# Two output blocks built in place of their summands, and the last entry's products reordered so that a plain copy comes last

## The chip, the cores and the metric

The kernel runs on one core of a Trainium2 chip. The metric is device time in microseconds for one execution, as the median of several runs. The core has TensorE (matrix products, PE in the profile; its weight loads are PEld), VectorE (DVE), ScalarE (ACT) and GpSimd (POOL). They run side by side, each through its own list of instructions in order, and wait for each other by semaphores. SyncE (SP) issues the transfers between memory and the core.

## The reference

The reference is attention through 32 packed queries per head, followed by a gated feed-forward layer that mixes over the sequence:

```
p_packed = softmax(p k^T / 8) v                       # per entry (8) and head (8)
x        = softmax(q p_packed^T / 8) p_packed         # 576 rows x 512
h        = relu(x @ w_in);  u, v = halves of h        # 512 + 512 columns
v_n      = (v - mean(v)) / sqrt(var(v) + 1e-6)        # per row
v_s      = w_spatial @ v_n + b_spatial                # mixes the 576 rows
out      = (u * v_s) @ w_out                          # 512 x 512
```

The change touches the last line alone, the product with `w_out`.

## The kernel before

The kernel goes through the eight entries of the batch one after the other (loop at line 1108 for entries 1 to 7; entry 0 is written out ahead of it). For each entry there is an `Attention` object, and a `FeedForward` object `ff` for the second half. While the products of one entry run, parts of the attention of later entries are put between them (`nxt`, `far`, `further`); for the last entry `nxt` is None and nothing is left to put there. The instructions of TensorE, VectorE, ScalarE and GpSimd stay in the order in which they are written (`InOrder`, `PIN`). The stores and loads are issued by SyncE, in one queue.

fp32 products are made from fp32r matmuls: an operand is split into a high part (`block_hi`, a rounding copy on ScalarE) and a low part (`block_lo`, a subtraction on VectorE), and each product sums high*high, high*low and low*high. In `product` (line 718) that is 12 matmuls of 128x288: for each half `f` of the output first four that read the high part of the moving operand, then two that read its low part.

For entries 1 to 7 the product with `w_out` is not made of eight block products but of seven (the Winograd form of Strassen's scheme). The gated activations `u` form four blocks g11, g12, g21 and g22 (features x sequence halves), the weights A11, A12, A21, A22 with the sums S1 to S4, the activations the differences T1 to T4 (`block_sum`, line 686, each made from an earlier one: T2 from T1, T4 from T2). With P1 = A11 g11, the output blocks of 256 features x 288 positions are

- block 11 = P1 + A12 g21. Both products are summed in the same PSUM tile, so `out11` is only a copy on ScalarE.
- block 12 = U + S4 g22 (summed onto S1 T1), where U = P1 + S2 T2.
- block 21 = U + A22 T4 (summed onto S3 T3).
- block 22 = U + P57, where P57 = S1 T1 + S3 T3; both are in the core's memory (SBUF).

P1, P5 and P57 live in one tile `prod` with the tag `v_h`, U in one with the tag `v_l` (`part`, line 741). The pool has one buffer for each of these tags. The next entry uses the same memory for its tiles `v_h` and `v_l`, the parts of the normalised activations, which it writes in `norm_hi` and `norm_lo`.

Each output block is made in an `o` tile (`out_block`, line 759, two buffers, tag "o") and stored from it by `put` (line 762):

```python
        def out_block(self):
            return two.tile([P, 2, HS], F32, tag="o", name="o")
```

A buffer is free again when the store that reads it has landed. Per entry four output blocks and the small tile `part` of the next entry's `relu(2)` (line 550, first instruction of ScalarE there) go through the two buffers in turn. The last lines of an entry are 1212 to 1250: after the seventh product (`A22`) entries 1 to 6 make block 22, then block 21; the last entry makes block 21 in two halves, each stored by itself, and then block 22.

The PSUM tiles of the four accumulators are `on(turns[0])` to `on(turns[3])`, that is all eight banks; each half `f` of a product lies in a bank of its own.

Of the kernel before, what the change touches and what calls it, by code (L numbers as in the profile page):

```python
# [14 lines left out]
ALU = mybir.AluOpType  # L15
# [8 lines left out]
HS = S // 2  # L24
# [25 lines left out]
def body(ctx: ExitStack, tc, q, k, v, vt, p, w_in, w_sp, b_sp, w_out, out):  # L50
# [11 lines left out]
    pe, dve, act, pool = (  # L62
        InOrder(tc, e) if x in PIN else e
        for e, x in ((nc.tensor, "t"), (nc.vector, "v"), (nc.scalar, "s"), (nc.gpsimd, "g"))
    )
# [6 lines left out]
    psum = ctx.enter_context(tc.tile_pool(name="ps", bufs=1, space=bass.MemoryType.PSUM))  # L72

    def on(i):

        return lambda: psum.tile([P, 2, 512], F32, tag=f"ps{i}", name=f"ps{i}_t")

    def by_turns(*quarters):
        turn = itertools.cycle([on(i) for i in quarters])
        return lambda: next(turn)()  # L80
# [25 lines left out]
    def load_k(b):  # L106
        pT = two.tile([P, NJ * NP], F32, tag="pT", name="pT")
        nc.sync.dma_start(pT, p[:, b, :])
        loaded["p", b] = pT
        kT = io.tile([P, 2, NJ, HS], F32, tag="kT", name="kT")  # L110
        for x in parts(b):
            nc.sync.dma_start(kT[:, x], k[b, :, x])
        loaded["k", b] = kT

    def load_v(b):
        v_sb = io.tile([P, NC + 1, H * D], F32, tag="v", name="v_sb")
        nc.sync.dma_start(v_sb[:, :NC, :], v[b])
        nc.sync.dma_start(v_sb[:TAIL, NC, :], vt[b])
        loaded["v", b] = v_sb

    def load_q(b):
        qT = io.tile([P, 2, NJ, HS], F32, tag="qT", name="qT")
        for x in parts(b):
            nc.sync.dma_start(qT[:, x], q[b, :, x])
        loaded["q", b] = qT
# [105 lines left out]
    A11, A12, A22, S1, S2, S3, S4, A21 = range(8)  # L231
# [265 lines left out]
    class FeedForward:  # L497
# [268 lines left out]
        def out_whole(self, k, f, t):  # L766
            o = self.out_block()
            act.copy(o, self.ds[k][:, :, :HS])
            self.put(o, f, t)

        def out11(self):
            self.out_whole(A12, 0, 0)

# [2 lines left out]
            self.add_part(o, "U", S4)  # L776
            self.put(o, 0, 1)

        def out21(self, fs=slice(0, 2)):
            if fs.start == 0:  # L780
                self.o21 = self.out_block()
            self.add_part(self.o21, "U", A22, fs)
            self.put(self.o21, 1, 0, fs)

        def out22(self):
            o = self.out_block()
            dve.tensor_tensor(o, self.part("U"), self.part("P57"), op=ALU.add)
            self.put(o, 1, 1)

# [15 lines left out]
    att, nxt, far, further = (Attention(b) for b in range(4))  # L807
    keep_warm(2, 9)
    att.pack_scores(by_turns(0, 3))
    ff = FeedForward(0, att)  # L810
# [297 lines left out]
    for b in range(1, B):  # L1108
        att, nxt, far = nxt, far, further
        further = Attention(b + 3) if b + 3 < B else None  # L1110
        ff = FeedForward(b, att)
        ff.value(2, psum=on(q0))
        ff.value(0, psum=on(q1))
        ff.relu(2)
        ff.value(1, psum=on(q2))
        ff.relu(0)
        ff.relu_tail()
        ff.stats(2)
        ff.inverse(2)
        ff.stats(0)  # L1120
        ff.inverse(0)
        ff.relu(1)
        if far:
            far.pack_turn(on(q3), ff.ps[2])
        if nxt:
            nxt.packed_turn(ff.ps[2])
            nxt.packed_turned()
        if far:
            far.pack_turned()
        ff.stats(1)  # L1130
        ff.inverse(1)
        ff.norm(2)
        ff.norm(0)
        ff.up(0, psum=on(q1))
        ff.up_relu(0)
        ff.norm_hi(0)
        ff.norm(1)
        ff.norm_lo(0)
        ff.up(1, psum=on(q2))
        ff.norm_hi(2)  # L1140
        ff.up_relu(1)
        ff.up(2, psum=on(q0))
        ff.up_relu(2)
        ff.tail_hi()
        ff.norm_lo(2)
        ff.up(3, psum=on(q3))
        ff.up_relu(3)
        ff.norm_hi(1)
        if nxt:
            nxt.query_scores(psum=by_turns(q1, q2))  # L1150
            nxt.query_tiles()
            if far:
                load_q(b + 2)
            nxt.mix(1, psum=on(q0))
            nxt.query_spread(0)
            nxt.query_spread(1)
            nxt.mix_hi(1)
            if far:
                far.pack_values(on(q3))
                far.packed()  # L1160
                if further:
                    load_v(b + 3)
            nxt.mix_lo(1)
        ff.norm_lo(1)
        if nxt:
            nxt.mix(0, psum=on(q1))
            nxt.mix_hi(0)
            if further:
                further.pack_scores(psum=by_turns(q2, q3))
                if b + 4 < B:  # L1170
                    load_k(b + 4)
                for r in range(2):
                    further.pack_max(r)
                    further.pack_exp(r)
            nxt.mix_lo(0)
            nxt.query_max(0)
            nxt.query_sub(0)
            nxt.query_exp(0)
            if further:
                further.pack_sum()  # L1180
        if further:
            turns = (q0, q1, q2, q3)
        else:
            turns = (q3, q2, q0, q1) if nxt else (q1, q2, q0, q3)
        if not nxt:
            for cs in ((0, 1), (2, 3)):
                ff.gate((0, 1), "hm", cs, psum=by_turns(*turns[:2]))
        for e, i in enumerate(turns):
            ff.gate((e,), "hmlt" if nxt or e > 1 else "lt", psum=on(i))
            if nxt and e == 1:  # L1190
                nxt.query_sum(0)
                nxt.query_norm(0)
            ff.gated(e)
            if nxt and e == 0:
                nxt.query_max(1)
                nxt.query_sub(1)
                nxt.query_exp(1)
            elif e == 1:
                ff.block_hi("g11")
                ff.block_sum("T1")  # L1200
                ff.block_hi("T1")
                ff.block_lo("g11")
                if nxt:
                    nxt.query_turn(0)
                    nxt.query_hi(0)
                ff.block_lo("T1")
            elif nxt and e == 2:
                nxt.query_lo(0)
                nxt.query_tail(0)
                nxt.query_sum(1)  # L1210
                nxt.query_norm(1)
        ff.product(A11, "g11", psum=on(turns[0]))
        ff.block_hi("g21")
        ff.block_sum("T3")
        ff.block_lo("g21")
        ff.keep_part("P1", A11)
        ff.block_hi("g22")
        ff.block_sum("T2")
        ff.product(S1, "T1", psum=on(turns[1]))
        ff.block_hi("T3")  # L1220
        ff.block_lo("g22")
        ff.keep_part("P5", S1)
        ff.block_lo("T3")
        ff.block_hi("T2")
        ff.product(A12, "g21", onto=A11)
        ff.out11()
        ff.block_sum("T4")
        ff.block_lo("T2")
        ff.block_hi("T4")
        ff.product(S4, "g22", onto=S1)  # L1230
        ff.block_lo("T4")
        if nxt:
            nxt.query_turn(1)
            nxt.query_hi(1)
        ff.product(S3, "T3", psum=on(turns[2]))
        ff.add_part("P57", "P5", S3)
        if nxt:
            nxt.query_lo(1)
            nxt.query_tail(1)
        ff.product(S2, "T2", psum=on(turns[3]))  # L1240
        ff.add_part("U", "P1", S2)
        ff.out12()
        ff.product(A22, "T4", onto=S3)
        if nxt:
            ff.out22()
            ff.out21()
        else:
            for f in range(2):
                ff.out21(slice(f, f + 1))
            ff.out22()  # L1250
        q0, q1, q2, q3 = turns[0], turns[1], turns[3], turns[2]


# [52 lines left out]
```

## Time and profile before

| what | us |
|---|---|
| median of three timed runs (408.6 to 409.56) | 409.43 |
| profiled execution, its own time | 407.98 |
| its span | 406.2 |
| TensorE busy (matmul) | 394.9 |
| VectorE busy | 332.9 |
| ScalarE busy | 192.7 |
| GpSimd busy | 74.1 |

The span counts from the first instruction of the program to its last; the profiled execution's own time is 1.78 us longer than the span. The granted TensorE clock was 0.996 of full speed over the execution. Matmuls overlap, so the duration of one (0.29 us) is longer than the time from one start to the next (0.13 us); the starts are what counts. In a row of the timeline the first number is the start in us from the span's start, the second the duration; where several instructions of one kind follow closely they are merged, with their count behind the x.

### The profile page before, as it was taken

To read this page: it belongs to the slowest core of one execution; us is meant where nothing else is said; L and a number is where in the kernel's file an instruction comes from. 1 tells how busy PE (TensorE), PEld (TensorE's weight loads), DVE (VectorE), ACT (ScalarE), POOL (GpSimd) and SP (SyncE) were. 2 spreads that over 40 slices of the span, in tenths; PEclk is the share of its full clock that TensorE was granted. 3 is DMA by queue.
4 is the path that set the end of the run, shared out by engine and by line. 5 is a ranking of instruction groups with operands and counts; after the bars stand their busy time and mean duration, and the time that the engine had idled before them with its cause. 6 is when DMAs were issued, how large, how long until landed. Compare 5 with 4: busy or idle time off the path is not lost.

```text
span 406.2 us, 8936 instructions
## 1 busy us (share of the span) xinstructions
PE 394.9 (97%) x3800; PEld 354.5 (87%) x3800; DVE 332.9 (82%) x567; ACT 192.7 (47%) x291; POOL 74.1 (18%) x98
## 2 busy tenths in 40 slices
PE   7999999999999999999999999999999999999993
PEld 5768977799799879999699888999799889999993
DVE  2597799979799779977899788995899789978563
ACT  3587865766435353434634273244634272526140
POOL 1566445644000120002100030001200030004000
PEclk9999999999999999999999999999999999999998
DMA  7999057730810227020530205002300200020002
GB/s 306 382 383 397 20 178 305 241 116 2 293 66 31 87 81 278 2 85 34 224 129 31 87 13 225 0 29 89 120 0 30 87 2 2 0 102 17 2 30 88
DMA packets 16620, 46.62 MB, mean 115 GB/s; under 512 B 1346, under 2 KB 10562, under 8 KB 13764
## 3 DMA queue, kind: packets, MB, share of 16 engines
q1 hardware_dynamic: 16580, 46.05, 31.1%
q8 instruction: 30, 0.49, 0.5%
q14 instruction: 10, 0.08, 0.1%
HBM read 36.61 MB, written 9.44 MB: 113 GB/s over the span
## 4 chain that ended last, share of the span: by engine, by line
PE 94%; DVE 3%; POOL 1%; issue 1%; DMA 1%; POOLq 0%; DVEq 0%
PE ps_t L43 94%; DVE nmax L43 1%; POOL bits L43 1%; DMA out_t<-o 1%; DVE bits L43 0%; DVE t L43 0%; DVE o L43 0%; DVE sm_t L43 0%; DVE w_in_sb L43 0%; DVE pp L43 0%; DVE mx L43 0%; DVE prod L43 0%; POOL ident masks.py:199 0%; DVE rtot L43 0%; POOL ident masks.py:197 0%
## 5 line engine op out<-in xcount | busy, mean ns | idle before, releaser
L43 PE MATMUL ps_t<-wsp_h,v_h 128*128 128x288 f32 x256 | 55.9, 300 | 0.0
L43 PE MATMUL ps_t<-wsp_l,v_h 128*128 128x288 f32 x256 | 54.5, 295 | 0.0
L43 POOL TENSOR_TENSOR rstd<-mv,eps 128x2 f32<-128x2 f32 (+2 forms) x26 | 6.9, 265 | 245.5 <-DVE mv L43 245.4
L43 PE MATMUL ps_t<-t,wout_h 128*128 128x288 f32 x232 | 48.3, 294 | 0.0
L43 PEld LDWEIGHTS ps_t<-wsp_h,v_h 128*128 128x128 f32 x256 | 40.8, 188 | 3.8 <-DVE m_l L43 1.9
L43 PEld LDWEIGHTS ps_t<-wsp_l,v_h 128*128 128x128 f32 x256 | 41.5, 189 | 0.0
L43 ACT CAST g_h<-u 128x576 fp32r<-128x576 f32 x24 | 16.1, 674 | 49.4 <-DVE u L43 49.1
L43 PE MATMUL ps_t<-wsp_h,v_l 128*128 128x288 f32 x256 | 39.4, 296 | 0.0
L43 PEld LDWEIGHTS ps_t<-t,wout_h 128*128 128x128 f32 x232 | 38.0, 188 | 0.0
L43 PEld LDWEIGHTS ps_t<-wsp_h,v_l 128*128 128x128 f32 x256 | 35.9, 189 | 0.5 <-issue 0.5
L43 PE MATMUL ps_t<-t,wout_l 128*128 128x288 f32 x116 | 32.3, 294 | 0.0
L43 PE MATMUL ps_t<-g_h,wout_h 128*128 128x288 f32 x104 | 30.1, 305 | 0.6 <-DVE pp L43 0.6
L43 PE MATMUL ps_t<-g_h,wout_l 128*128 128x288 f32 x104 | 29.1, 295 | 0.0
L43 PE MATMUL ps_t<-a_h,m_h 128*128 128x288 f32 x128 | 28.1, 301 | 0.0
L43 PE MATMUL ps_t<-a_h,m_l 128*128 128x288 f32 x128 | 27.4, 296 | 0.0
L43 PE MATMUL ps_t<-a_l,m_h 128*128 128x288 f32 x128 | 27.4, 296 | 0.0
L43 DVE TENSOR_TENSOR u<-ps_t,u 128x576 f32<-128x576 f32 x28 | 21.0, 749 | 7.3 <-PE ps_t L43 7.3
L43 PE MATMUL ps_t<-m_l,a_h 128*128 128x512 f32 x80 | 25.8, 390 | 0.0
L43 PE MATMUL ps_t<-m_h,a_h 128*128 128x512 f32 x80 | 25.8, 391 | 0.0
L43 ACT ACTIVATE sm_t<-sm_t 128x576 f32<-128x576 f32 x16 | 11.0, 685 | 27.5 <-DVE sm_t L43 23.7
L43 DVE TENSOR_TENSOR o<-ps_t,prod 128x576 f32<-128x576 f32 (+1 forms) x15 | 10.7, 717 | 15.4 <-DMA out_t<-o 15.1
L43 ACT COPY part<-ps_t 64x512 f32<-64x512 f32 x8 | 4.7, 583 | 39.2 <-DVE o L43 39.2
(136 smaller groups left out, 989.6 us busy)
## 6 DMA issues: line engine op xcount, KB each, us to landing
out_t<-o SPq DMA_DIRECT2D x31, 288.0 KB, 2.3
v_sb<-in_v SPq DMA_DIRECT2D x8, 1024.0 KB, 8.1
qT<-in_q SPq DMA_DIRECT2D x7, 1152.0 KB, 5.4
kT<-in_k SPq DMA_DIRECT2D x7, 1152.0 KB, 8.4
raw<-in_w_in SPq DMA_DIRECT2D x4, 1024.0 KB, 12.7
raw<-in_w_out SPq DMA_DIRECT2D x2, 1024.0 KB, 9.8
kT<-in_k SPq DMA_DIRECT2D x2, 576.0 KB
qT<-in_q SPq DMA_DIRECT2D x2, 576.0 KB, 12.8
```

The lines of the kernel that those rows point to most:

```text
L43: return lambda *a, **k: self.tc.keep_in_program_order(call(*a, **k))
```

## The change

`out22` adds U into P57 in place and stores from there; `out21` adds the seventh product into U in place and stores from there. Neither takes an `o` tile any more. Blocks 11 and 12 still do. The end of an entry moves into two methods: `down` for entries 1 to 6, in the order of before, and `last_down` for entry 7, in another order: the products are A11, S1, S2, S3, S4, A22, A12 (before: A11, S1, A12, S4, S3, S2, A22), the splits and sums follow that order, the stores go 12, 22, 21, and block 11 comes last, copied and stored in two halves (`out11_split`).

```diff
+        def out11_split(self):
+            o = self.out_block()
+            for i in range(2):
+                act.copy(o[:, i], self.ds[A12][:, i, :HS])
+                self.put(o, 0, 0, slice(i, i + 1))
...
-        def out21(self, fs=slice(0, 2)):
-            if fs.start == 0:
-                self.o21 = self.out_block()
-            self.add_part(self.o21, "U", A22, fs)
-            self.put(self.o21, 1, 0, fs)
+        def out21(self):
+
+            o = self.part("U")
+            self.add_part(o, "U", A22)
+            self.put(o, 1, 0)
 
         def out22(self):
-            o = self.out_block()
-            dve.tensor_tensor(o, self.part("U"), self.part("P57"), op=ALU.add)
+
+            o = self.part("P57")
+            dve.tensor_tensor(o, self.part("U"), o, op=ALU.add)
             self.put(o, 1, 1)
+
+        def down(self, turns, nxt):
...
+            self.product(A22, "T4", onto=S3)
+            self.out22()
+            self.out21()
+
+        def last_down(self, turns):
+
+            self.product(A11, "g11", psum=on(turns[0]))
+            self.block_sum("T2")
+            self.block_hi("T2")
+            self.block_sum("T3")
+            self.block_hi("T3")
+            self.block_lo("T2")
+            self.keep_part("P1", A11)
+            self.product(S1, "T1", psum=on(turns[1]))
+            self.block_hi("g22")
+            self.block_lo("T3")
+            self.block_lo("g22")
+            self.keep_part("P5", S1)
+            self.block_sum("T4")
+            self.block_hi("T4")
+            self.product(S2, "T2", psum=on(turns[3]))
+            self.add_part("U", "P1", S2)
+            self.block_hi("g21")
+            self.product(S3, "T3", psum=on(turns[2]))
+            self.block_lo("T4")
+            self.add_part("P57", "P5", S3)
+            self.block_lo("g21")
+            self.product(S4, "g22", onto=S1)
+            self.out12()
+            self.out22()
+            self.product(A22, "T4", onto=S3)
+            self.out21()
+            self.product(A12, "g21", onto=A11)
+            self.out11_split()
...
         if nxt:
-            ff.out22()
-            ff.out21()
+            ff.down(turns, nxt)
         else:
-            for f in range(2):
-                ff.out21(slice(f, f + 1))
-            ff.out22()
+            ff.last_down(turns)
```

## Rows read from the trace of the kernel before

**Rows 1.** The page, busy us by engine, share of the span, instructions.
```profile
PE 394.9 (97%) x3800; PEld 354.5 (87%) x3800; DVE 332.9 (82%) x567; ACT 192.7 (47%) x291; POOL 74.1 (18%) x98
```

**Rows 2.** The chain that ended last: start us, us, what.
```profile
74.13 324.15 PE ps_t L43 x2922
...
399.87 2.26 DMA out_t<-o
...
402.23 0.76 DVE o L43
```

**Rows 3.** Waits of VectorE, whole run: us in total, times, longest.
```profile
DVE o L43 <- DMA out_t<-o: 16.6, 7, 4.1
```

**Rows 4.** Timeline, VectorE and ScalarE, from entry 6 to entry 7.
```profile
363.52 0.76 DVE L43 TENSOR_TENSOR o<-ps_t,prod 128x576 f32<-128x576 f32 x1 [1.75 <-DMA out_t<-o]
364.29 0.58 ACT L43 COPY part<-ps_t 64x512 f32<-64x512 f32 x1 [5.70 <-DVE o L43]
367.49 1.03 ACT L43 ACTIVATE vr<-ps_t 128x1024 f32<-128x1024 f32 x1 [1.56 <-PE ps_t L43]
371.48 1.06 ACT L43 CAST v_h<-vr 128x1024 fp32r<-128x1024 f32 x1 [1.75 <-DVE vr L43]
372.57 1.23 DVE L43 TENSOR_TENSOR v_l<-vr,v_h 128x1024 fp32r<-128x1024 f32 x1
```

**Rows 5.** Waits of TensorE's weight loads, whole run.
```profile
PEld ps_t L43 <- DVE m_l L43: 1.9, 4, 0.5
```

**Rows 6.** Stores into the output tensor, from 393 us on.
```profile
DMA to landing us min/median/max: 2.1/2.2/2.2
```

**Rows 7.** Timeline, TensorE: second product's first matmul, last product's last two.
```profile
390.19 0.29 PE L43 MATMUL ps_t<-t,wout_h 128*128 128x288 f32 x1
...
399.41 0.43 PE L43 MATMUL ps_t<-t,wout_h 128*128 128x288 f32 x2
```

**Rows 8.** Timeline, VectorE and ScalarE: splits, spacings, copies, a reader of a product.
```profile
282.95 0.37 ACT L43 COPY p1T<-ps_t 64x256 f32<-64x256 f32 x1 [0.82 <-DVE ppT L43]
...
382.14 0.76 DVE L43 TENSOR_TENSOR g<-u 128x576 f32<-128x576 f32 x1
382.98 0.67 ACT L43 CAST t<-g 128x576 fp32r<-128x576 f32 x1 [0.17 <-DVE g L43]
383.69 0.76 DVE L43 TENSOR_TENSOR t<-g,t 128x576 fp32r<-128x576 f32 x1
...
389.60 0.76 DVE L43 TENSOR_TENSOR u<-u 128x576 f32<-128x576 f32 x1
390.31 0.76 DVE L43 TENSOR_TENSOR g_l<-u,g_h 128x576 fp32r<-128x576 f32 x1
390.45 0.64 ACT L43 COPY prod<-ps_t 128x576 f32<-128x576 f32 x1 [0.17 <-PE ps_t L43]
390.98 0.75 DVE L43 TENSOR_TENSOR g<-u,g 128x576 f32<-128x576 f32 x1
390.99 0.68 ACT L43 CAST g_h<-u 128x576 fp32r<-128x576 f32 x1
391.56 0.67 ACT L43 CAST t<-u 128x576 fp32r<-128x576 f32 x1
...
396.71 0.76 DVE L43 TENSOR_TENSOR prod<-ps_t,prod 128x576 f32<-128x576 f32 x1 [1.16 <-PE ps_t L43]
```

**Rows 9.** Timeline, SyncE's queue: the last three stores.
```profile
400.36 0.89 SPq L764 DMA_DIRECT2D out_t<-o  x2
403.02 0.38 SPq L764 DMA_DIRECT2D out_t<-o  x1
```

**Rows 10.** Stretches at the end: us, busy us by engine, clock, DMA share, GB/s.
```profile
401.00:401.50 0.50, 0.00 (x0) 0.00 (x0) 0.00 (x0) 0.00 (x0) 0.00 (x0) 1.00 1.03 357
...
403.50:404.00 0.50, 0.00 (x0) 0.00 (x0) 0.00 (x0) 0.00 (x0) 0.00 (x0) 0.50 0.13 44
...
404.50:405.00 0.50, 0.00 (x0) 0.00 (x0) 0.00 (x0) 0.00 (x0) 0.00 (x0) 0.50 0.55 189
```

More of the change, by code (lines that the diff above doesn't have):

```diff
@@ L788, in out22 @@
             self.put(o, 1, 1)
+        def down(self, turns, nxt):
[13 more added lines that the diff above has]
+            self.product(A12, "g21", onto=A11)
+            self.out11()
+            self.block_sum("T4")
[3 more added lines that the diff above has]
+            self.block_lo("T4")
+            nxt.query_turn(1)
+            nxt.query_hi(1)
+            self.product(S3, "T3", psum=on(turns[2]))
+            self.add_part("P57", "P5", S3)
+            nxt.query_lo(1)
+            nxt.query_tail(1)
+            self.product(S2, "T2", psum=on(turns[3]))
[4 more added lines that the diff above has]
+            self.out21()
@@ new lines, in last_down @@
+        def last_down(self, turns):
+            self.product(A11, "g11", psum=on(turns[0]))
+            self.block_sum("T2")
+            self.block_hi("T2")
+            self.block_sum("T3")
+            self.block_hi("T3")
+            self.block_lo("T2")
+            self.keep_part("P1", A11)
+            self.product(S1, "T1", psum=on(turns[1]))
+            self.block_hi("g22")
+            self.block_lo("T3")
+            self.block_lo("g22")
+            self.keep_part("P5", S1)
+            self.block_sum("T4")
+            self.block_hi("T4")
+            self.product(S2, "T2", psum=on(turns[3]))
+            self.add_part("U", "P1", S2)
+            self.block_hi("g21")
+            self.product(S3, "T3", psum=on(turns[2]))
+            self.block_lo("T4")
+            self.add_part("P57", "P5", S3)
+            self.block_lo("g21")
+            self.product(S4, "g22", onto=S1)
+            self.out12()
+            self.out22()
+            self.product(A22, "T4", onto=S3)
+            self.out21()
+            self.product(A12, "g21", onto=A11)
+            self.out11_split()
@@ L1211, in body @@
                 nxt.query_norm(1)
[L1212 to L1231, printed above, removed]
-        if nxt:
[L1233 to L1244, printed above, removed]
-            ff.out22()
-            ff.out21()
-        else:
-            for f in range(2):
-                ff.out21(slice(f, f + 1))
-            ff.out22()
+        if nxt:
+            ff.down(turns, nxt)
+        else:
+            ff.last_down(turns)
         q0, q1, q2, q3 = turns[0], turns[1], turns[3], turns[2]
```

## The prediction

> **What bounds the kernel now.** I read the busy shares first, then the chain of waits over the whole run, then the waits of each engine, and last the two stretches that the change touches: the passage from one entry to the next, and the end. TensorE is busy for 394.9 of 406.2 us [rows 1]. The chain says more than the share: from 74.13 us to 398.27 us it is one unbroken piece of 2922 matmuls, 324.15 us long [rows 2]. So from entry 1 on only matmul time counts, and VectorE, ScalarE and the stores are hidden, until the last products are done. Then the chain leaves TensorE: VectorE adds, a store from `o` that takes 2.26 us to land, and after it one more VectorE add, at 402.23 us, whose store closes the run [rows 2]. That add makes block 22. The `o` tiles have two buffers, block 22 gets the one that block 12 was stored from, and it waits until that store is in memory. The same wait stands once in each of the entries 1 to 7, 16.6 us in all [rows 3], but in six of the seven TensorE is at work on the next entry meanwhile.
>
> **The change part by part.** (a) Entries 1 to 6, blocks 22 and 21 made in `P57` and `U` instead of `o`. No instruction is added: two adds of 128x576 stay two adds, two stores stay two. What goes is the wait for the landing (1.75 us before the add at 363.52, entry 6) and with it the later start of `part` on ScalarE at 364.29 [rows 4]. Does anything gain by it? ScalarE's second relu of the next entry, at 367.49, waits for TensorE after 1.56 us of idleness [rows 4]. So whatever ScalarE and VectorE gain earlier they give back there, and the norms that follow are as late as before. TensorE itself stands on no part of this in the chain [rows 2]. I cost it at 0. Bounds: TensorE's weight loads wait 1.9 us in four places for VectorE's `m_l` [rows 5]; if an earlier VectorE took all of that away it would be -1.9 us. Upwards: the stores now read tiles whose memory is next written as `v_h` (ScalarE, 371.48) and `v_l` (VectorE, 372.57) [rows 4]; a store issued when the add ends, some 2 us before that of today's 364.28, lands after about 2.2 us [rows 6], 7 us before 371.48. So 0, and I take 0, the value of the chain's row.
>
> (b) The last entry's products in another order. Seven products of 12 matmuls stay seven. The second starts at 390.19 and the last matmul at 399.41 + 0.13 = 399.54, so the next would be at 399.67; six products in 9.48 us are 1.58 each [rows 7]. The starts are 388.61, 390.19, 391.77, 393.35, 394.93, 396.51, 398.09. Now A11, S1, S2, S3, S4, A22, A12 stand in these places. TensorE's end does not move if every operand is in time. An operand's high part is wanted at the start, its low part by the fifth matmul, 0.53 later. The first new operand is T2, wanted at 391.77 and 392.30. The trace has the same step for T1: sum at 382.14, high part on ScalarE at 382.98 (0.08 after the sum's end), low part at 383.69 (0.04 after the high part's end), done at 384.45 [rows 8]. T2's sum takes the place of today's first sum at 389.60 [rows 8]; so its high part is done at 391.12 and its low part at 391.92. The margins are 0.65 and 0.38 us.
>
> The rest by the spacings of independent neighbours, 0.67 on VectorE (390.31 to 390.98) and 0.57 on ScalarE (390.99 to 391.56) [rows 8]. ScalarE: T2 high 390.44, T3 high 391.11, P1 391.68, g22 high 392.25, P5 392.82. VectorE: T3 sum 390.27, T2 low 391.16, T3 low 391.83, g22 low 392.97 (after its high part), T4 sum 393.64, U 394.31, T4 low 395.20 (T4 high 394.48 to 395.16), P57 395.87, g21 low 396.54, block 12 397.21, block 22 397.88, block 21 398.55 to 399.31. Each product is out when its reader comes: a reader can start 0.20 after the next product starts (396.71 after 396.51) [rows 7, 8]. T3, g22, T4 and g21 have their low parts at 392.6, 393.7, 396.0 and 397.3, against 393.9, 395.5, 397.0 and 398.6. So no stall; stall cost 0, but VectorE is now 0.5 us behind TensorE where blocks 12, 22 and 21 are made.
>
> (c) The end. After TensorE's last matmul only ScalarE's copy of one half of block 11, 128x288, is left. The trace has no such copy. From 64x256 in 0.37 us below and 128x576 in about 0.65 above (ScalarE's `P1` copy; the copy `part`, 64x512, takes 0.58) [rows 4, 8], I take 0.40, since 288 columns are nearest to 256. TensorE ends at 399.54 + 0.30 = 399.84, the copy at about 400.30. SyncE issues its stores at least 0.49 apart (two in 0.89, the second 0.40 long) [rows 9]: block 12 at 398.00, block 22 at 398.67, block 21 at 399.34, the first half of 11 at 399.83, the second at 400.32. That is 2.70 us before today's last issue, 403.02 [rows 9].
>
> But five stores now follow closely. Today's last store, issued at 403.02, has data moving from 403.94 (share 0.13 in the half microsecond to 404) to 404.78 (0.55 of the half from 404.5) [rows 10]: 0.92 us to the first byte, 0.84 for 288 KB, and at a landing time of 2.2 [rows 6] some 0.46 from the last byte to landing. With block 12 issued at 398.00, data starts at 398.92, and four blocks' worth (12, 22, 21 and two halves) need 4 x 0.84 = 3.36 us in line: 402.28. Landing is 402.74; the run ends 0.95 after that, as 406.2 stands to 405.25 today: 403.7. So the span shrinks by 2.5 us. Alone in the queue the last half would land 2.2 after 400.32, the span would shrink by 2.7: that is the lower end of the time. The upper end comes from VectorE, since the queue now starts with block 12: half a microsecond more delay there makes the saving 2.0.
>
> *A rule against the split.* In the trace two halves of block 21 are stored 0.49 apart, and behind a whole block the queue moved 357 GB/s in the half microsecond from 401.0 [rows 9, 10]: halves cost the queue no extra time. The Trainium skill, page "DMA: Bandwidth & Descriptors", section "Measured (HBM→SBUF, 128 partitions, SWDGE, issued from GpSimd)", wants DMAs of 1 MiB or more, and its section "Anatomy of one DMA — SWDGE (gpsimd) path" gives each a fixed 2.0 us; taken as paid one after the other, a split store would cost, by an estimate from that page, one more 2.0 us, and the gain would be 0.5. The trace does not agree: it overlaps all but the data.
>
> **The sum.** Entries 1 to 6: 0. Products of the last entry: 0. End: -2.5. The profiled execution took 407.98 us, 1.78 more than its span; it becomes 405.5. The median of the three timed runs is 409.43, 1.45 above the profiled one; the same difference gives 406.9. That is 0.6% less.
>
> **The rivals.**
> The middle gains too (8%): with VectorE no longer held up, the four waits for `m_l` go: 2.5 + 1.9 = 4.4, so 405.0. For it: those waits are on TensorE's loader [rows 5]. Against: the chain shows no break there [rows 2], and ScalarE waits for TensorE right after the passage [rows 4].
> The new order stalls TensorE or holds up VectorE (13%): T2's margin is 0.38 us [rows 8], less than one instruction's spacing on ScalarE (0.57). One copy that comes in between makes T2 late by 0.2, and every reader after it; one such slip in each of the three sums takes 0.6 from TensorE and about as much from VectorE's line of blocks: the saving falls to 1.3 or less, so 408.1 or more.
> Slower (3%): the stores out of `U` and `P57` hold memory of which there is one buffer. ScalarE's write to `v_h` at 371.48 would wait for the landing, and the gates behind it on TensorE. The price: to be over 0.3% slower, six passages must lose (2.5 + 1.2) / 6 = 0.6 us each, 410.7 or more. It decides only when the landing comes after 371.48, about 9 us after the issue; landings take 2.2 [rows 6], and the longest wait for one is 4.1 [rows 3].
> That the change doesn't do what it says: if the adds into `U` and `P57` were ordered behind something else than their operands, block 22 would still wait and the end would stay; nothing in the names shows such a thing, and it is in the 13%.
>
> **How the numbers follow.** The forecast has 76%: 406.9, with its own range 406.6 to 407.4 (savings of 2.8 to 2.0). The measurement tells 0.3%, 1.2 us, from no change. The forecast and the extra gain are faster, and a quarter of the stall case: 87%; the rest of that case is 10% within 0.3%; 3% slower. The range, with the 0.96 us by which the three runs before differ, is 405.7 to 408.1.
>
> **What would show it.** Right: no wait of VectorE's `o` for a store anywhere; the last matmul at the same place, about 399.5; a ScalarE copy of 128x288 last, about 0.4 long, near 399.9; the last store issued near 400.3, data in one unbroken stretch of about 3.4 us before the end. Wrong: gaps in TensorE between 391.7 and 399.8; a passage between entries that is shorter or longer than before; a last store issued well after the last copy; a span above 405.

## The result, and the profile after

The changed kernel takes 404.41 us (median of four runs, 404.32 to 404.80) against 409.34 for the one before (408.60 to 409.56). The ratio is 0.9885, with a 95% interval of 0.9868 to 0.9902: 1.15% faster. Forecast were 406.9 and 0.6%, with a range down to 405.7. The sign and the end of the run were right; a second gain, about as large as two thirds of the first, was taken for nothing.

The two profiled executions differ less than the medians: 407.98 and 404.37 us, spans 406.2 and 402.6. The first line is the page of the changed kernel [rows 1], the others are the last pieces of its chain [rows 2].

```profile
PE 393.5 (98%) x3800; PEld 354.0 (88%) x3800; DVE 333.7 (83%) x566; ACT 193.5 (48%) x292; POOL 74.2 (18%) x98
...
351.73 47.21 PE ps_t L43 x332
398.94 0.02 issue
398.96 0.40 ACT o L43
399.36 0.30 ACTq L1338
```

At the end the chain leaves TensorE at 398.94, for a copy on ScalarE; no landing of a store stands in it any more. (From 332.64 to 351.73, inside entry 6, it also runs over VectorE and ScalarE. It does so in a second execution of the kernel before too, and entry 6 is as long as it was.) From the last matmul's start to the end of the span it was 406.21 - 399.54 = 6.67 us [rows 7]; it is 402.59 - 398.63 = 3.96 now, 2.7 less. The timeline of that end, VectorE, ScalarE and SyncE (start, duration):

```profile
395.96 0.75 DVE L43 TENSOR_TENSOR o<-ps_t,prod 128x576 f32<-128x576 f32 x1
396.63 0.75 DVE L43 TENSOR_TENSOR prod<-prod 128x576 f32<-128x576 f32 x1
396.74 0.37 SPq L764 DMA_DIRECT2D out_t<-o  x1
397.41 0.37 SPq L764 DMA_DIRECT2D out_t<-prod  x1
397.48 0.76 DVE L43 TENSOR_TENSOR prod<-ps_t,prod 128x576 f32<-128x576 f32 x1
398.96 0.70 ACT L43 COPY o<-ps_t 128x288 f32<-128x288 f32 x2 [4.46 <-PE ps_t L43]
399.38 0.84 SPq L764 DMA_DIRECT2D out_t<-o  x2
```

Blocks 12, 22 and 21 follow each other without a wait and are done before TensorE; both copies of block 11 stand behind its last matmul.

The last matmul itself comes 0.91 us earlier (399.54 to 398.63), although TensorE's list only got another order. That is the gain that the forecast missed. It is in the passages between entries. These are the first matmuls of entries 3 and 4, before and after, and `part`, ScalarE's first copy of entry 3:

```profile
179.77 0.40 PE L43 MATMUL ps_t<-m_h,a_h 128*128 128x512 f32 x1
185.46 0.58 ACT L43 COPY part<-ps_t 64x512 f32<-64x512 f32 x1 [8.03 <-DVE o L43]
226.76 0.39 PE L43 MATMUL ps_t<-m_h,a_h 128*128 128x512 f32 x1
```
```profile
179.91 0.39 PE L43 MATMUL ps_t<-m_h,a_h 128*128 128x512 f32 x1
181.07 0.59 ACT L43 COPY part<-ps_t 64x512 f32<-64x512 f32 x1 [3.50 <-PE ps_t L43]
226.25 0.39 PE L43 MATMUL ps_t<-m_h,a_h 128*128 128x512 f32 x1
```

Before, `part` came 5.69 us after the entry's first matmul and the entry took 46.99 us; now it comes after 1.16 and the entry takes 46.34. Entry 5 is the same case (5.60 and 45.42; 1.16 and 44.85). Entries 2, 4 and 6 had `part` after 3.4 us and are as long before as after. So the two entries whose wait was the longest (4.1 and 4.0 us, the 4.1 of [rows 3]) lost 0.65 and 0.57 us, 1.2 together; the start of the run is 0.1 later, and TensorE's last entry 0.2 longer (38.61 to 38.79 us), which gives the 0.9.

What `part` waits for is not the add on VectorE that its row names. It takes the buffer that block 22 was stored from, and by the trace's semaphores it starts 0.10 us after that store has landed, in entry 3 (185.36) as in the other passages. Block 22's store follows 0.66 us behind block 12's, for which the add of block 21 waits; so both come late together.

Where TensorE lost it, in entry 3 before: its loader waits for ScalarE's `u` in the middle of the query scores, because ScalarE empties the PSUM tiles late (its three copies `u` start only at 194.02). The rows of ScalarE show why nothing was given back on the way: behind the late `part` both relus of the entry (output `vr`) follow without an idle moment, while in the changed kernel the second of them waits for TensorE for 1.70 us (second fence).

```profile
186.06 1.94 ACT L43 ACTIVATE vr<-ps_t 128x1024 f32<-128x1024 f32 x2
...
194.02 1.70 ACT L43 ACTIVATE u<-ps_t 128x576 f32<-128x576 f32 x3
194.70 0.64 PEld L43 LDWEIGHTS ps_t<-qT,ppT 64*32 64x32 f32 x16 [0.25 <-ACT u L43]
```
```profile
186.47 1.03 ACT L43 ACTIVATE vr<-ps_t 128x1024 f32<-128x1024 f32 x1 [1.70 <-PE ps_t L43]
```

The chain of before counted this stretch as unbroken TensorE [rows 2], since its matmuls only move apart there and none of the gaps shows as an idle wait of the engine.

Why two of the stores landed late is in the view of the transfers. First the stretch of entry 3 before, 179.9 to 184.7 us (40 slices of 0.12 us: GB/s; then queues and issues), then entry 4, 226.9 to 229.3 (40 slices of 0.06 us):

```profile
GB/s 0 0 0 0 0 0 0 0 173 365 317 317 259 365 482 336 336 375 346 288 336 317 87 10 19 38 38 38 19 10 19 29 19 29 19 29 19 19 29 19
...
q8 instruction: 1, 0.02, 1.7%
q14 instruction: 1, 0.01, 0.6%
...
out_t<-o SPq DMA_DIRECT2D x2, 288.0 KB, 4.7
```
```profile
GB/s 0 0 0 0 0 0 0 0 0 0 0 0 0 0 0 0 134 326 403 326 365 326 346 307 288 326 346 461 326 365 346 365 365 346 346 346 346 346 403 346
...
out_t<-o SPq DMA_DIRECT2D x2, 288.0 KB, 2.3
```

In entry 3 the bulk of both blocks has moved after 1.7 us, at some 340 GB/s, and then 10 to 40 GB/s go on for two more: about one of 16 engines is still at work. The steps of the store's semaphore say the same: of the 16 for block 12 in entry 3, 15 come by 182.23 and the last at 184.59; in entry 4 all 16 come between 229.07 and 229.22. Two transfers of a kind of their own ("instruction", 16 and 8 KB) stand in that stretch, and none in entry 4's. Of the larger sort the page lists 30 over the run, 0.49 MB, for the 7600 instructions of TensorE and its loader [rows 1]. The Trainium skill, page "DMA: Bandwidth & Descriptors", section "Why a DMA increments its semaphore by 16 and not by 1", says that the engines of one DMA finish independently and that only the count of all of them means landed; the trace agrees: the tail of one engine made 4.7 us out of 2.3.

### The profile page after: what moved, and what is told of

Read it like the earlier page. It is cut to its first block, busy times and chain, and to the rows that moved or that the text cites. A ratio compares the mean times of both kernels' runs of the same rounds, so it can differ in the third digit from the quotient of the medians.

```text
span 402.6 us, 8936 instructions
## 1 busy us (share of the span) xinstructions
PE 393.5 (98%) x3800; PEld 354.0 (88%) x3800; DVE 333.7 (83%) x566; ACT 193.5 (48%) x292; POOL 74.2 (18%) x98
## 4 chain that ended last, share of the span: by engine, by line
PE 89%; DVE 6%; DMA 1%; ACT 1%; issue 1%; POOL 1%; SPq 0%; ACTq 0%; POOLq 0%
PE ps_t L43 89%; DMA kT<-in_k 1%; DVE sm_t L43 1%; DVE u L43 1%; DVE nmax L43 1%; POOL bits L43 1%; DVE m_l L43 1%; DVE sm L43 1%; DVE t L43 1%; DVE mx L43 1%; ACT p L43 0%; DVE w_in_sb L43 0%; DVE v_l L43 0%; ACT raw L43 0%; ACT m_h L43 0%
## 5 line engine op out<-in xcount | busy, mean ns | idle before, releaser
L43 ACT ACTIVATE vr<-ps_t 128x1024 f32<-128x1024 f32 (+1 forms) x18 | 16.7, 932 | 26.8 <-PE ps_t L43 26.8
L43 DVE BATCH_NORM_STATS2 bn<-vr 128x6 f32<-128x512 f32 x32 | 20.7, 682 | 9.7 <-ACT vr L43 9.6
```

The costliest lines, as they stand in the source:

```text
L43: return lambda *a, **k: self.tc.keep_in_program_order(call(*a, **k))
```

## The experiments

Two theories. A: the passages count. A store of block 12 lands late where a fetch of TensorE's instructions falls on it; the add of block 21 waits for it, and `part` for the store of block 22 right behind it; beyond some delay TensorE pays. B: the passages are worth nothing, as forecast, and the rest lies at the start or the end. In the figures below "delay" is `part` after the first matmul of its entry, "length" the time from there to the next entry's first matmul (for entry 7 to its last).

**The kernel before once more** (no edit).

> The kernel before, unchanged, for another profiled execution of it. Theory A (late landings: in some of the six passages between entries a store of block 12 lands some 2 us later than usual, block 21's add and the next entry's first ScalarE copy wait for it, and TensorE then loses about 0.55 us at the next query scores): ratio 1.000; a profile whose time is near the median of 409.3 has four or five passages with a wait of about 4 us instead of the two of the first profile, one nearer to 408.0 has two. Rival B (the passages are worth nothing and the rest of the difference lies at the start or the end of the run): the profile's time differs from the first one with the same number of long waits, and the difference is found before 74 us or after 398 us.

Ratio 1.0005 (0.9991 to 1.0019). Its ten runs go from 406.94 to 409.23, those of the kernel before beside it from 407.26 to 409.32, while the changed kernel stayed within 0.5 us. The profiled execution took 409.06 and has three long waits, 18.2 us of waits in all instead of 16.6; the third is before the last entry, where the first profile had 1.75:

```profile
360.10 0.39 PE L43 MATMUL ps_t<-m_h,a_h 128*128 128x512 f32 x1
365.00 0.76 DVE L43 TENSOR_TENSOR o<-ps_t,prod 128x576 f32<-128x576 f32 x1 [4.06 <-DMA out_t<-o]
365.74 0.58 ACT L43 COPY part<-ps_t 64x512 f32<-64x512 f32 x1 [7.98 <-DMA out_t<-o]
...
400.49 0.43 PE L43 MATMUL ps_t<-t,wout_h 128*128 128x288 f32 x2
```

A delay of 5.64 us, and the last entry's matmuls take 40.52 us instead of 38.61. `part` starts here while the add of block 21 is still running, so it cannot have waited for that. The chain of this execution leaves TensorE at this place and shows the whole path: the add of block 22, the landing of its store, `part`, the norms, and only then TensorE again:

```profile
360.19 0.76 DVE o L43
...
360.96 4.68 DMA out_t<-o
...
365.74 0.59 ACT part L43
...
375.81 0.94 ACT v_h L43
...
376.80 1.32 PE ps_t L43 x8
```

So two executions of one kernel differ by how many landings are hit; here it is three, fewer than the four or five that theory A had put down.

**Middle alone, end alone.**

```diff
# in place in entries 1 to 6, last entry as before (the second run has it the other way round)
         if nxt:
             ff.down(turns, nxt)
         else:
-            ff.last_down(turns)
+            ff.last_old(turns)     # 1212 to 1250 of before, blocks in o tiles
```

> Entries 1 to 6 as in the changed kernel (blocks 22 and 21 in place), the last entry as before. Theory A: no passage waits for a landing any more, TensorE's start of the last products comes about 1.1 us earlier than in the first profile of before, time 409.3 - 2.2 = 407.1, ratio 0.995. Rival B (the forecast's zero for the middle): 409.3, ratio 1.000.

Ratio 0.9958 (0.9944 to 0.9973): 1.7 us, 406.81. No wait for a landing is left but the one at the end, and the entries are as long as in the changed kernel.

```profile
DVE o L43 <- DMA out_t<-o: 1.5, 1, 1.5
```

> Entries 1 to 6 as before (blocks 22 and 21 made in o tiles), the last entry as in the changed kernel. Theory A: only the end gains, 2.7 us, time 406.7, ratio 0.993, with two or more long waits in the passages. Rival B: all of the gain is here, 404.4, ratio 0.988.

Ratio 0.9935 (0.9916 to 0.9955): 2.7 us; last matmul to end 4.24 us. B falls with both. The two parts add to 1.07%, against 1.15% for the whole; the difference is inside the intervals.

**Own buffers instead of in place.** Blocks 22 and 21 each get an `o` tile that nothing else uses.

```diff
-                self.o21 = self.out_block()
+                self.o21 = outs.tile([P, 2, HS], F32, tag="o21", name="o")
...
-            o = self.out_block()
+            o = outs.tile([P, 2, HS], F32, tag="o22", name="o")
```

> The kernel before, with blocks 22 and 21 in o tiles of their own buffers (one each), so that no add waits for the store of block 12 or 11; order and number of instructions as before, nothing in place. Theory A (the wait is the cause, not the place of the sum): the passages gain as in the changed kernel, 2.2; the end loses its wait for one landing but keeps the old order, stores of 12, 21 and 22 in line behind each other, 1.5 less; 409.3 - 3.7 = 405.6, ratio 0.991. Rival C (in-place adds are what helps): 409.3 or near.

Ratio 0.9929 (0.9907 to 0.9950), 405.40 us. VectorE waits for no landing, delays 1.15 to 1.18 and entries as short as in the changed kernel; last matmul to end 5.21, 1.46 less than before. Rival C falls: what helps is that nothing waits for the stores of blocks 12 and 22.

**The end in its two parts.** One kernel keeps the old order and makes the blocks in place, the other keeps the `o` tiles and takes the new order (both in the last entry alone).

> Entries 1 to 6 as before; in the last entry blocks 22 and 21 in place, products in the old order, stores 12, 22, 21 in two halves. If the order of the products gives the end only a part, the wait alone goes: after TensorE's end block 22 and two halves of 21 are still added, and four stores' data stand in line from 0.92 us after block 12's issue: 1.5 us less than before, 406.9 against 408.4, ratio 0.996. If the wait were all of the end's gain: 2.7 less, 0.9935 as with the whole new end.

> Entries 1 to 6 as before; in the last entry the new order with block 11 last, but blocks 22 and 21 in o tiles, so block 21 waits for the store of 12 and block 11 for that of 22. If both parts of the end are needed: 1.45 us less than before, ratio 0.9965. If the order alone were enough: 2.7 less, 0.9935.

Ratios 0.9951 (0.9935 to 0.9968) and 0.9978 (0.9955 to 1.0001). From the last matmul to the end it is 5.24 us in place (-1.43) and 5.57 with the new order (-1.10); both together 4.24 (-2.43, from the run with the end alone), about the sum of the two. The second interval touches no change at all, so what the order alone gives is read from the trace and not from the times. In that kernel the chain goes through a landing again: block 21's add waits for the store of block 12, and block 11's copies stand behind it:

```profile
397.39 0.76 DVE o L43
398.17 2.53 DMA out_t<-o
400.81 0.77 DVE o L43
401.69 0.40 ACT o L43
```

Neither is enough: in place alone leaves adds behind TensorE, the order alone leaves the wait.

**More stores, to lengthen the wait.** In entries 1 to 6 block 12 is stored four times.

```diff
             self.put(o, 0, 1)
+            if 0 < self.b < B - 1:
+                for _ in range(3):
+                    self.put(o, 0, 1)
```

> The kernel before, with the store of block 12 repeated three times in entries 1 to 6 (same data, same place, about 0.85 us of transfer each), so that block 21's add waits some 4.3 us in every passage. Theory A (a wait of 1.75 us is hidden, one over 3.5 us costs TensorE about 0.6 to 1.0): all six passages lose, 0.8 in each of five and 1.2 before the last entry, 5.2 in all against 1.7 in the typical run of before: 408.4 + 3.5 = 411.9, ratio 1.0085. Rival B (waits in the passages are hidden whatever their length): 408.4, ratio 1.000.

> The changed kernel with the same three more stores of block 12 in entries 1 to 6. Theory A: nothing waits for these stores any more, so no passage loses: 404.4, ratio to the kernel before 0.990, and TensorE's passages as long as in the changed kernel. If the transfers themselves slow something (loads behind them, the next blocks' stores): more than 405.5.

Ratio 1.0376 (1.0332 to 1.0419) for the kernel before: 424.51 us, far more than the 411.9 of A. The delays became longer than foreseen, 6.5 to 9.0, and by another way. In the passage into entry 2 the stores go out at 134.34 (block 12), 135.00 (block 22, 0.03 after its add has ended), 136.63 (block 12 again, once the first has landed), 138.34 (block 21), 138.90 and 141.43. By the semaphores block 21's add now takes the buffer of block 22, as that of block 12 is held by its further stores, and waits for block 22's landing (2.58 us, ending at 137.56), and `part` waits for the landing of block 21's store, behind the add: two landings in a row instead of one. The changed kernel with the same stores has 0.9900 (0.9874 to 0.9926) and no entry more than 0.2 us longer: with nothing waiting, it hardly notices them. The traces put together show how the delay turns into time:

| entry | delay, length (us), by run |
|---|---|
| 3 | 1.16, 46.34 (changed); 5.03, 46.35 (new order with `o`); 5.29, 46.59 (before again); 5.69, 46.99 (before); 8.84, 50.92 (more stores) |
| 5 | 1.16, 44.85 (changed); 3.38, 44.85 (in place, old order); 5.18, 45.00 (before again); 5.60, 45.42 (before); 6.67, 46.48 (more stores) |
| 6 | 1.16, 42.42 (changed); 3.36, 42.43 (before); 4.97, 43.49 (28 products, below); 6.67, 45.21 (more stores) |
| 7 | 1.15, 38.60 (middle alone); 3.36, 38.61 (before); 5.08, 39.96 (48 products, below); 5.64, 40.52 (before again); 9.04, 44.13 (more stores) |

Up to an edge the delay costs nothing, beyond it one us per us, as far as 2.8 us beyond. The edge is at about 5.0 us in entries 3 and 5, 3.9 in entry 6 and 3.7 in entry 7. The usual delay of before, 3.4, lies 1.6 from the first and only 0.5 and 0.4 from the other two. The two longest delays, 8.84 and 9.04, do not show the slope: there TensorE stood long, and afterwards its granted clock was 0.50 for a while, 1.2 instead of 2.4 GHz. These are two stretches of entry 3 in that run (us; busy us of TensorE, its loader, VectorE, ScalarE and GpSimd; clock; DMA share; GB/s):

```profile
188.80:192.40 3.60, 1.07 (x9) 0.83 (x8) 0.67 (x1) 1.26 (x2) 0.00 (x0) 1.00 0.49 168
193.20:196.50 3.30, 3.30 (x15) 3.30 (x15) 3.27 (x10) 2.39 (x4) 1.61 (x4) 0.50 0.11 41
```

In the second one matmuls start 0.24 us apart instead of 0.13, and about 1.5 of the 4.6 us that the entry lost fall there. Entry 7 of that run has the same (0.50 from 384.30 to 387.60, after TensorE had done nothing from 380.0 to 383.4).

**Moving the fetches.** Warm-up products ahead of everything push TensorE's list of instructions along without touching an entry.

```diff
     load_k(0)
+    keep_warm(1, 48)        # 28 and 14 in the other two
     att, nxt, far, further = (Attention(b) for b in range(4))
```

> The kernel before with 48 more warm-up products (96 more instructions of TensorE and its loader) ahead of everything; its time is not compared, since the start is longer. If the late landings come from the fetches of TensorE's own instructions, which run on the same transfer engines at fixed places of its instruction list, then 96 instructions more move them: the passages into entries 4 and 6 get the late landing (fetches about 1.6 and 1.2 us after block 12's issue), and those into 3 and 5 get none. If late landings belong to the place of the entry (its loads, its addresses): into 3 and 5 as before.

> The kernel before with 28 more warm-up products (56 instructions). By the fetch theory no passage has a fetch within the landing of block 12's store, so no wait of 4 us anywhere and the passages are as short as in the changed kernel: 1.7 us less there, against some 2 us more at the start, ratio near 1.000; what counts is the trace. By the rival (the place of the entry): into 3 and 5 a wait of about 4 us.

In both the waits of about 4 us left entries 3 and 5 (with 48 products entry 5 keeps one of 2.3), but for others than named: with 48 products entry 2 (3.2 us) and entry 7 (3.5), with 28 products entry 4 (3.7) and entry 6 (3.4). The page of that profile gives the reason: 3896 matmuls with 48 more, so each product is two matmuls and two weight loads, and the shifts were 192 and 112 instructions, twice what was counted. By the old trace 112 bring fetches near the stores of entries 4 and 6, and 192 near that of entry 7 (entry 2's store comes out nearest at about 160, so the places hold to a few tens of instructions). An instruction transfer of 16 KB stands in the stretch of each; this is entry 6 with 28 products, 324.9 to 328.9 us:

```profile
q8 instruction: 1, 0.02, 1.5%
...
out_t<-o SPq DMA_DIRECT2D x1, 288.0 KB, 4.0
```

The timed ratio with 28 products, 1.0113 (1.0092 to 1.0133), tells nothing of this, since the start grew by more than the 2 us foreseen. With the right count a shift that hits no entry was named ahead:

> The kernel before with 14 more warm-up products. The profile counts two matmuls and two weight loads for each such product (3896 matmuls with 48 more), so this is 56 instructions, the number that the two runs before were meant to straddle. Fetch theory: no instruction fetch within the landing of block 12's store, so all six passages wait 1.7 to 1.8 us and none is longer than in the changed kernel; the start is some 3 us longer, which is not compared. Rival (the place of the entry, or chance): at least one or two waits of more than 3.4 us.

No wait over 1.8 us, in an otherwise unchanged kernel, and each entry but one within 0.1 us of the changed kernel's length or shorter (entry 6: 42.56 against 42.42):

```profile
DVE o L43 <- DMA out_t<-o: 12.1, 7, 1.8
```

So it is the place in TensorE's list that makes a landing late, not the entry. The place is not exact: each shift was profiled once, and the fetch near entry 7 fell on the store in one execution of the kernel before and ended 0.1 us ahead of its issue in the other; with 14 products the fetch in entry 3 had ended 0.4 us before block 12's store went out. What does not depend on this is the count over all fifteen traces, with six passages each. In 30 of the 90 a 16 KB instruction transfer starts between 0.9 and 2.3 us after the issue of block 12's store, and in all 30 that store or block 22's took 3.6 us or more to land. In the other 60 none took more than 3.01, and the five that took 2.88 to 3.01 have an 8 KB one in their stretch.

**Two tries at a shorter end.** First the halves of block 11 taken apart, each copied and stored behind its own six matmuls:

```diff
-            self.product(A12, "g21", onto=A11)
-            self.out11_split()
+            o = self.out_block()
+            for f in range(2):
+                self.product(A12, "g21", onto=A11, fs=(f,))
+                act.copy(o[:, f], self.ds[A12][:, f, :HS])
+                self.put(o, 0, 0, slice(f, f + 1))
```

> The changed kernel with block 11's two halves taken apart: product of half 0, its copy and its store, then product of half 1, its copy and its store. In the changed kernel both copies stand after TensorE's last matmul. If the wait of the first copy is for its half alone: the first copy runs beside the second half's matmuls, the last store is issued 0.4 us earlier, 404.0, ratio 0.9895 to 0.9905 with before at 408.4. If the product's second half then waits for the copy (one tile, one wait): TensorE stops 0.5 us and nothing is gained, 404.4 or more.

Ratio 0.9908 (0.9892 to 0.9924), 405.12 us: no gain. The first copy is early, but the second half's first matmul waits for its end, since the two halves are one PSUM tile:

```profile
398.40 0.40 ACT L43 COPY o<-ps_t 128x288 f32<-128x288 f32 x1 [3.68 <-PE ps_t L43]
398.85 0.40 PE L43 MATMUL ps_t<-g_h,wout_h 128*128 128x288 f32 x1 [0.49 <-ACT o L43]
```

Then the second half in a tile of its own, added to P1 by VectorE (`product(..., psum=on(turns[3]), fs=(1,), to="x")`):

> The changed kernel; in the last entry the second half of A12 g21 goes into a PSUM tile of its own (that of S2, long read) and is added to P1 by VectorE, so that the first half's copy need not wait for it, nor it for the copy. If the one-tile wait of the run before was all that stood against the early half: TensorE without a stop, the first copy 0.8 us before TensorE's end, the last store issued 0.4 us earlier than in the changed kernel, 0.4 us less: 404.1, ratio 0.988 with before at 408.9. Otherwise 404.4 or more.

```profile
398.26 0.40 ACT L43 COPY o<-ps_t 128x288 f32<-128x288 f32 x1 [3.71 <-PE ps_t L43]
399.06 0.46 DVE L43 TENSOR_TENSOR o<-ps_t,prod 128x288 f32<-128x288 f32 x1 [0.77 <-PE ps_t L43]
399.55 0.34 SPq L764 DMA_DIRECT2D out_t<-o  x1
```

TensorE does not stop and the last store goes out 0.27 us earlier than in the changed kernel (399.82), but it lands after 2.0 instead of 1.8 us, as the stores ahead of it are still in line. Ratio 0.9907 (0.9883 to 0.9930), 404.85 us: no better than the changed kernel, which stays the best here.

## Why the prediction was wrong, step by step

- **(a), the passages, failed.** The step reads "whatever ScalarE and VectorE gain earlier they give back there ... I cost it at 0". It was taken from the passage into entry 7 with its wait of 1.75 us [rows 4]. That passage is indeed free. But the row of waits held a longest one of 4.1 us [rows 3], and it was used only as a bound on landings against the next write of `v_h`, never followed through to TensorE. The idle 1.56 us of ScalarE [rows 4], on which "give back" rests, is cover for the usual delay alone: in entry 3 the long wait used it up, and ScalarE's relus had no idle time left. Followed, in entry 3: `part` 5.69 us after the first matmul, the copies `u` late, the query scores stretched, 0.65 us lost. The entries 3 and 5 gave 1.2 in the profiled pair; timed, the middle alone gave 0.42% (0.27 to 0.56), 1.7 us. A passage shorter than before was among the signs of being wrong that the prediction itself had named. It also tied `part` to the add of block 21, as the row's label says; it waits for the landing of block 22's store.
- **The first rival was near in size and wrong in mechanism.** It gave the middle 1.9 us, 8% chance, through the waits for `m_l` [rows 5]. Those are unchanged after (1.9 us, four times). What went, in entries 3 and 5, was the wait for PSUM tiles at the query scores.
- **The chain as witness.** "TensorE itself stands on no part of this in the chain" [rows 2] leaned on a piece that stays unbroken while its matmuls move apart; their ends are modelled. Comparing the lengths of equal entries in that same trace (46.99 against 46.3 for entries 3 and 4) would have shown the loss. In the second execution of the same kernel the chain does leave TensorE, by the landing before the last entry.
- **(b), the new order, nearly right.** T2 came in time. The last entry is 0.2 us longer all the same; all of it is at the start of the A22 product, whose first two matmuls start 0.24 and 0.21 us after their neighbours instead of 0.13, just after VectorE's P57 add (394.63 to 395.38) has read the PSUM tile that it adds onto. That read was not among the steps; that it is the cause was not tried.
- **(c), the end, right in size**: 2.7 us against 2.5. Its parts moved. Block 12 was stored 0.36 us earlier against TensorE's end than worked out (2.20 before it instead of 1.84). The last issue came 0.40 later (0.88 after TensorE's end instead of 0.48), because the first copy waited for the whole product and not for its half. Both together loosened the line of stores (the engines' share was 0.73 to 0.99 between 400.2 and 400.8) before the last half, which landed 1.81 us after its issue, the 0.92 + 0.42 + 0.46 of a half block alone. Other traces with this end have 3.85 and 4.24 us behind the last matmul's start instead of 3.96, so the agreement to 0.2 is no closer than the traces are to each other. The copy took the 0.40 estimated. The rule on batching of the Trainium skill (page "DMA: Bandwidth & Descriptors", sections "Measured (HBM→SBUF, 128 partitions, SWDGE, issued from GpSimd)" and "Anatomy of one DMA — SWDGE (gpsimd) path", for transfers issued by GpSimd), by which an estimated 0.5 of the gain would have been left, is not borne out here by the 1.81 us nor by the 2.7 us gained.
- **The run before as a base.** Its profiled execution was one of its quick ones, 1.4 us under the median. The spread of that kernel comes at least in part from the number of landings that are hit, and the change takes that away. What part of the 1.4 us this makes is open: starts of the run differ by up to 1.4 us from one trace to the next (first product with `w_out` of entry 0 between 73.96 and 75.35). The stated range does not follow from its own parts either: 406.6 and 407.4, widened by 0.96, are 405.6 and 408.4, not 405.7 and 408.1. The measured 404.41 lies below both.

## What to carry to other kernels

When a wait repeats once per stage, look at its longest instance, not the usual one, and follow that one to the engine that counts; compare the lengths of equal stages, for a busy share and an unbroken chain hide a pipeline that stretches. A buffer that is free only when a store has landed ties compute to the slowest of 16 transfer engines; make the result in the place of a summand or in a tile of its own, and the landing time stops to matter. At the end of a run both are wanted: no wait for a landing, and the operation with the least work behind TensorE last.

## What the runs showed of the hardware

Fetches of TensorE's own instructions (30 of 16 KB, 0.49 MB over the run) share the engines with the stores. One that falls on a store of block 12 raises its landing from 2.3 us to as much as 4.6, by one of the 16 engines alone (15 steps of the semaphore by 182.23, the last at 184.59). Its place follows from the position in TensorE's list, to some tens of instructions: with 14 more warm-up products none of the six passages was hit, with 28 and 48 others than before. In the changed kernel the landings are still hit (3.8 to 4.2 us in entries 3 and 5), only nothing waits for them. Where TensorE stood long (busy 1.07 of 3.60 us), the clock granted to it afterwards was 0.50.
